# 512 tokens as the moving operand of layer two's output products, with shifted attention steps, reordered low parts and shared reciprocals

## The chip, the cores and the metric

One core of a Trainium2 chip runs the whole program. The metric is device time in microseconds (us); each kernel is timed by the median of several runs. A separate run, taken by the hardware profiler, gives the profile, and its time stands beside the others.

## What is computed

Attention over 4 batches, 8 heads, 512 local and 32 global tokens, then two feed-forward layers on the resulting 2176 rows of 512 columns. The local tokens see a window of 32 to either side and the global tokens; the global tokens see all.

```python
k_all = np.concatenate([k_g, k_l], axis=2);  v_all = np.concatenate([v_g, v_l], axis=2)
out_g = sm(scale * q_g @ k_all.T) @ v_all
mask = np.abs(pos[:, None] - pos[None, :]) <= window          # window = 32
s_l = np.concatenate([scale * q_l @ k_g.T, np.where(mask, scale * q_l @ k_l.T, -1e9)], axis=-1)
out_l = sm(s_l) @ v_all                                       # sm: exp(s - max) / (sum + 1e-9)
x = rows of out_g and out_l, heads side by side               # 2176 x 512
h = x @ w_in;   x = (maximum(h, 0) + alpha * minimum(h, 0)) @ w_out      # 512 -> 2048 -> 512
h = x @ w2_in;  out = (h * clip(h + 3, 0, 6) / 6) @ w2_out               # 512 -> 2048 -> 512
```

## The kernel before

**Precision.** Matmuls of the two layers run on float32r operands. Every operand is split into a high part (its cast to float32r) and a low part (the rest), and a product of two operands is three matmuls: high with high, low weight with high data, high weight with low data. The weights reach the chip as 64-bit floats and are made into 32-bit ones and split on the way (L114 to L138).

**Layer one** goes through the tokens in five blocks of 512, 512, 512, 256 and 384 columns (tokens stand in the columns). In each of a block's steps `h_tile` (L590) makes the hidden values of 128 rows of the 2048 in a bank `h_ps`, 12 matmuls; `act` (L600 to L609) turns them on ScalarE (ACT) and VectorE (DVE) into a high and a low part `g`; and `y_tiles` (L621) adds them, two steps later, to four banks `y_ps`, again 12 matmuls. In block 0 the weights are converted as they arrive, and its first eight steps take half the columns each. At the end of a block `x_transposed` (L550) turns the attention rows `xo` of the next block on TensorE (PE) into banks `xt_ps`, and `x_split` (L562, L563) makes the parts `xt` of them.

**Attention** is laid between these steps. Its work is 32 units (a batch, half of its tokens, two heads), taken in pairs. For a pair, `scores` (L234) makes 32 small matmuls into two banks; `softmax` masks them and finds the largest (L260), takes exponentials with their sums (L265), adds 1e-9 (L267) and takes reciprocals (L269), unit by unit; the probabilities are turned, by PE for the first pairs, later by DVE (L285) and a trip through DRAM; `values` (L299) makes 32 more (a float32 matmul counts twice in the trace) and multiplies by the reciprocals. Three tables set when: `STARTS` the step at which a pair's scores go (from pair 4 on), `WAITS` how many steps later its values go, and `STEPS` how many attention steps are taken behind each `h_tile`. The global tokens' attention follows in the last block.

**Layer two** takes its 2048 local tokens in two groups of 1024 (each a pair of 512-column halves), by Strassen's method in Winograd's form. Seven products of a quarter of the size take the place of eight, once for the hidden values and once for the output. The **input products** (`product`, L947) hold 128x128 weights stationary and move 512 tokens into banks `k_ps`. The **output products** (`summed`, L1035) are the other way round: seven sums `i` over four steps `k`, each of which makes a high and a low part of 512 tokens by two times 128 hidden rows (`parts_of`, L960 and L961: `gh`, `gl`), takes a tile `ws` of output weights that came from DRAM (`take`), and for two rows `jp`, four chunks of 128 tokens and three pairs of parts holds the chunk of tokens stationary and moves 256 output columns:

```python
bank = y[c // 2][:, 256 * (c % 2):256 * (c % 2) + 256]
mm = nc.tensor.matmul(bank, lhsT=part[:, jp, 128 * c:128 * c + 128],
                      rhs=wo[:, jp, 256 * wl:256 * wl + 256], ...)
```

So tokens come out on the partitions, as the rows of the output are. DVE adds up the sums (L877, tiles `res`), and `store` (L1062) writes each of four results per group by four transfers of 128 rows with 1 KB runs, from SyncE's queue (SP), which also fetches `ws`. The 128 global rows go by the plain method in the second group (L899, L911); `rest_out` (L920) uses the same `wo` tiles for them and adds to one bank `yr_ps`, and `rest_rows` stores it (L931, L934).

**Order.** The instructions of each engine are put in order when the program is built, by a scheduler that runs a timeline of its own; operations under `here` keep the order of the code. PSUM is two pools of four banks: `psy` holds `y_ps` in layer one, and `psr` serves everything else there (`h_ps`, scores, values, transposes), so that each needs a bank that ACT and DVE have emptied.

## Time and profile before

| | |
|---|---|
| median of 3 runs | 812.97 us (812.88 to 813.52) |
| the profiled execution | 818.06 us, of which 816.3 us are the span of the trace |
| PE busy | 795.4 us (97%), 6812 matmuls |
| DVE busy | 613.1 us (75%) |
| ACT busy | 409.8 us (50%) |
| GpSimd (POOL) busy | 86.6 us (11%) |
| mean granted clock of PE | 0.994 |

The trace has five stages: attention alone until about 20 us, layer one until 471, then in layer two the first group's input products to 549 and output products to 633, and the second group's input products to 716 and output products to 810. PE's busy time holds matmuls whose ends are modelled, and weight loads (PEld) overlap them; a pitch is better read from how long a known count took. The clock is given as a share of full speed, 1.0 for 2.4 GHz and 0.5 for 1.2 GHz. "Idle" is the time that an engine stood before an instruction, with what ended it.

### The profile page before, as it was taken

How to read it: one execution, taken by the hardware profiler on the slowest of the kernel's cores; microseconds unless marked ns; L12 is line 12 of the kernel's file. 1: busy time of each engine (PE TensorE's matmuls, PEld its weight loads, DVE VectorE, ACT ScalarE, POOL GpSimd, SP SyncE). 2: the span in 40 equal slices, each digit the busy share in tenths (PEclk: the TensorE clock that was granted, in tenths of full speed). 3: DMA queues.
4: the chain of work that ended last, by engine and by line, in shares of the span. 5: the costliest groups of instructions: out<-in, count | busy, mean ns of one | idle time of the engine just before them, and what ended most of it. 6: DMA issues, size and time to landing. Idle time of an engine off the chain costs nothing.

```text
span 816.3 us, 17563 instructions
## 1 busy us (share of the span) xinstructions
PE 795.4 (97%) x6812; PEld 696.2 (85%) x6812; DVE 613.1 (75%) x1307; ACT 409.8 (50%) x864; POOL 86.6 (11%) x141
## 2 busy tenths in 40 slices
PE   6999999999998999999999999999999999999998
PEld 4778777878886887788999988889999888899997
DVE  4889997678878887777899847778867576678443
ACT  5878886455546544544456434334543334333431
POOL 0332202122220322112000000000000000000000
PEclk9999999999999999999999999999999999999999
DMA  9978887489988889998995586676786666655663
GB/s 336 352 248 281 296 270 218 167 268 332 334 289 330 281 305 338 316 320 297 313 340 199 205 274 190 202 220 199 209 258 199 206 182 206 184 178 161 208 180 111
DMA packets 85507, 204.06 MB, mean 250 GB/s; under 512 B 8752, under 2 KB 31024, under 8 KB 85424
## 3 DMA queue, kind: packets, MB, share of 16 engines
q1 hardware_dynamic: 78112, 181.83, 67.2%
q0 software_dynamic: 7120, 20.98, 8.2%
q8 instruction: 54, 0.88, 0.5%
q14 instruction: 29, 0.24, 0.1%
q10 hardware_dynamic: 192, 0.13, 0.1%
HBM read 149.95 MB, written 52.95 MB: 249 GB/s over the span
## 4 chain that ended last, share of the span: by engine, by line
PE 79%; DMA 3%; DVE 1%; ACT 0%; issue 0%; SPq 0%; ACTq 0%
PE o_ps L1035 20%; PE k_ps L947 19%; PE y_ps L621 18%; PE h_ps L590 16%; DMA gk<-in_kN 2%; PE yr_ps L920 1%; PE hr_ps L899 1%; DMA xo<-turn 1%; PE o_ps L299 1%; PE s_ps L234 1%; PE gs_ps L440 1%; PE go_ps L477 0%; PE tr_ps L911 0%; PE xt_ps L550 0%; DVE p L260 0%
## 5 line engine op out<-in xcount | busy, mean ns | idle before, releaser
L590 PE MATMUL h_ps<-xt,wt 128*128 128x512 f32 (+2 forms) x1008 | 205.3, 353 | 2.4 <-DVE st L260 2.1
L621 PE MATMUL y_ps<-g,wt 128*128 128x512 f32 (+2 forms) x1008 | 206.4, 355 | 1.0 <-POOL wt L137 0.8
L590 PEld LDWEIGHTS h_ps<-xt,wt 128*128 128x128 f32 x1008 | 169.8, 191 | 25.8 <-issue 4.0
L621 PEld LDWEIGHTS y_ps<-g,wt 128*128 128x128 f32 x1008 | 168.8, 191 | 26.0 <-issue 2.4
L1035 PE MATMUL o_ps<-ws,gh 128*128 128x256 f32 x896 | 160.9, 283 | 0.1
L947 PE MATMUL k_ps<-bt,ws 128*128 128x512 f32 x672 | 157.2, 390 | 0.0
L947 PEld LDWEIGHTS k_ps<-bt,ws 128*128 128x128 f32 x672 | 124.6, 188 | 24.9
L1035 PEld LDWEIGHTS o_ps<-ws,gh 128*128 128x128 f32 x896 | 138.8, 192 | 0.6 <-issue 0.3
L1035 PE MATMUL o_ps<-ws,gl 128*128 128x256 f32 x448 | 124.2, 283 | 0.0
L961 DVE TENSOR_TENSOR gl<-far,gh 128x1024 fp32r<-128x1024 f32 x56 | 68.5, 1223 | 42.6 <-ACT gh L960 42.6
L960 ACT CAST gh<-far 128x1024 fp32r<-128x1024 f32 x56 | 58.7, 1049 | 74.7 <-PE o_ps L1035 70.9
L1035 PEld LDWEIGHTS o_ps<-ws,gl 128*128 128x128 f32 x448 | 84.9, 192 | 0.0
L881 ACT ACTIVATE t<-far,half_sb 128x512 f32<-128x512 f32 x48 | 34.8, 725 | 77.0 <-DVE far L877 77.0
L602 DVE SCALAR_TENSOR_TENSOR t<-t,c_sb,h_ps 128x512 f32<-128x512 f32 (+2 forms) x84 | 53.0, 641 | 17.9 <-ACT t L600 17.4
L600 ACT ACTIVATE t<-h_ps 128x512 f32<-128x512 f32 (+2 forms) x76 | 41.7, 550 | 47.0 <-PE h_ps L590 46.2
L608 ACT CAST g<-t 128x512 fp32r<-128x512 f32 (+2 forms) x76 | 43.7, 575 | 40.6 <-DVE t L602 37.7
L609 DVE TENSOR_TENSOR g<-t,g 128x512 fp32r<-128x512 f32 (+2 forms) x76 | 49.4, 653 | 10.9 <-ACT g L608 10.1
L265 ACT ACTIVATE p<-p,st 128x128 f32<-128x128 f32 x128 | 49.7, 392 | 10.0 <-DVE st L260 8.8
L114 ACT ACTIVATE raw<-raw,quarter_sb 128x512 uint32<-128x512 uint32 x64 | 49.2, 770 | 5.6 <-DMA raw<-in_w 5.6
L125 DVE SCALAR_TENSOR_TENSOR z<-z,raw 128x512 uint32<-128x512 uint32 x64 | 44.1, 695 | 5.0 <-ACT z L120 2.2
L127 DVE SCALAR_TENSOR_TENSOR z<-raw,z 128x512 uint32<-128x512 uint32 x64 | 44.7, 702 | 0.5
L882 DVE SCALAR_TENSOR_TENSOR far<-t,far 128x512 f32<-128x512 f32 x48 | 33.1, 689 | 11.8 <-ACT t L881 11.8
(110 smaller groups left out, 833.6 us busy)
## 6 DMA issues: line engine op xcount, KB each, us to landing
raw<-in_w SPq DMA_DIRECT2D x64, 512.0 KB, 7.1
ws<-wo SPq DMA_DIRECT2D x60, 512.0 KB, 3.9
ws<-wi SPq DMA_DIRECT2D x56, 512.0 KB, 4.7
v_t<-in_vE SPq DMA_DIRECT2D x32, 512.0 KB, 7.7
qk_t<-in_qkE SPq DMA_DIRECT2D x32, 368.0 KB, 5.7
wi<-raw SPq DMA_DIRECT2D x16, 512.0 KB, 5.4
wi<-parts SPq DMA_DIRECT2D x16, 512.0 KB, 6.3
wo<-raw SPq DMA_DIRECT2D x16, 512.0 KB, 5.8
```

Source lines behind the costliest of these rows:

```text
L114: here(nc.scalar.activation(low, low, AF.Relu, bias=quarter_sb, scale=0.9 * 2.0 ** -29))
L125: nc.vector.scalar_tensor_tensor(out=bits, in0=bits, scalar=3, in1=low, op0=ALU.logical_shift_left, op1=ALU.bitwise_or)
L127: nc.vector.scalar_tensor_tensor(out=bits, in0=high, scalar=0x80000000, in1=bits, op0=ALU.bitwise_and, op1=ALU.bitwise_or)
L265: nc.scalar.activation(to, to, AF.Exp, bias=st[:, 1, n:n + 1], scale=-1.0, accum_out=st[:, 2, n:n + 1])
L590: nc.tensor.matmul(ps[:, a:b], lhsT=wts[j][:, 0, wl, 128 * c:128 * c + 128], rhs=xt[c][:, xl, at:at + b - a], start=k == 0, stop=k == 3 * ...
L602: nc.vector.scalar_tensor_tensor(out=t[:, c:d], in0=t[:, c:d], scalar=c1_sb[:, j:j + 1], in1=ps[:, c:d], op0=ALU.mult, op1=ALU.add)
L609: nc.vector.tensor_tensor(out=g[:, 1, a:b], in0=t[:, a:b], in1=g[:, 0, a:b].bitcast(F32), op=ALU.subtract)
L621: nc.tensor.matmul(y[c][:, at:at + b - a], lhsT=wts[j][:, 1, wl, 128 * c:128 * c + 128], rhs=g[:, gl, a:b], start=first, stop=last, skip_g ...
L947: nc.tensor.matmul(bank, lhsT=wt[:, wl, 128 * c:128 * c + 128], rhs=bt[x][:, c, xl, 0:w], start=first and k == 0, stop=k == 5, skip_group_ ...
L960: nc.scalar.copy(hi, src)
L961: nc.vector.tensor_tensor(out=lo, in0=src, in1=hi.bitcast(F32), op=ALU.subtract)
L1035: mm = nc.tensor.matmul(bank, lhsT=part[:, jp, 128 * c:128 * c + 128], rhs=wo[:, jp, 256 * wl:256 * wl + 256], start=opens, stop=k == NP / ...
```

## The change

It has five parts.

1. **Output products.** `summed` holds 128x128 weights stationary (128 of the 256 output columns) and moves all 512 tokens of a part: 672 matmuls of 512 columns where there were 1344 of 256. Output columns now stand on the partitions and tokens in the columns. To bring the rows back, `store` has DVE turn each result in 32x32 squares, twice 128x512, and writes it by four transfers with runs of 64 columns (256 bytes). For that the columns of the output weights are permuted on the host, the copies and sums that fill a result write through a strided view (`half_of`), and the global rows read their weights through another (`in_order`).
2. **Attention steps.** Pair 13's scores go one step earlier (`STARTS`), with the values where they were; pair 5's values go one step later (`WAITS`).
3. **Shared reciprocals.** The two units of a pair share a tile of sums, and one addition and one reciprocal of 128x8 take the place of two of 128x4 each.
4. **Low parts last.** In layer one the matmul with the low part of the weights comes last of the three. `late`, in block 0's half steps, sorts it behind all the others of `h_tile`.
5. **Turning at a border.** `x_transposed` for the next block stands behind `y_tiles` of that step, and not ahead of it.

```diff
-STARTS = [0, 4, 8, 12, 16, 19, 22, 25, 29, 33, 36, 39]
+STARTS = [0, 4, 8, 12, 16, 19, 22, 25, 29, 32, 36, 39]
-WAITS = [4, 4, 5, 4, 5, 5, 5, 5, 5, 5, 5, 5]
+WAITS = [4, 5, 5, 4, 5, 5, 5, 5, 5, 6, 5, 5]
...
+            st = att.tile([128, 3, 8], F32, tag="st", name="st", bufs=4)
             for e, u in enumerate(us):
-                softmax(u, [x[:, 256 * e:256 * e + 256] for x in s])
-
-        def softmax(u, s):
+                softmax(u, [x[:, 256 * e:256 * e + 256] for x in s], st[:, :, 4 * e:4 * e + 4])
+            nc.vector.tensor_scalar(out=st[:, 2, :], in0=st[:, 1, :], scalar1=1e-9, scalar2=None, op0=ALU.add)
+            rs = att.tile([128, 8], F32, tag="rs", name="rs", bufs=FIRST_UNITS)
+            nc.vector.reciprocal(out=rs, in_=st[:, 2, :])
+            for e, u in enumerate(us):
+                rs_t[u] = rs[:, 4 * e:4 * e + 4]
+
+        def softmax(u, s, st):
...
-            nc.vector.tensor_scalar(out=st[:, 3, :], in0=st[:, 2, :], scalar1=1e-9, scalar2=None, op0=ALU.add)
-            rs_t[u] = att.tile([128, 4], F32, tag="rs", name="rs", bufs=FIRST_UNITS)
-            nc.vector.reciprocal(out=rs_t[u], in_=st[:, 3, :])
...
-    def h_tile(xt, wts, parts):
+    def h_tile(xt, wts, parts, late=False):
         ps = bank("h_ps")
         for a, b, j, at in parts:
-            k = 0
-            for c in range(NC):
-                for wl, xl in ((0, 0), (1, 0), (0, 1)):
...
+            steps = [(c, w) for c in range(NC) for w in ((0, 0), (0, 1), (1, 0))]
+            if late:
+                steps.sort(key=lambda step: step[1][0])
+            for k, (c, (wl, xl)) in enumerate(steps):
+                nc.tensor.matmul(ps[:, a:b], lhsT=wts[j][:, 0, wl, 128 * c:128 * c + 128],
+                                 rhs=xt[c][:, xl, at:at + b - a], start=k == 0, stop=k == 3 * NC - 1)
...
-            steps = [(w, c) for w in ((0, 0), (1, 0), (0, 1)) for c in range(len(y))]
+            steps = [(w, c) for w in ((0, 0), (0, 1), (1, 0)) for c in range(len(y))]
...
+        def in_order(w):
+            return w.rearrange("p (c b x) -> p b c x", c=2, b=4)
...
-                                     rhs=wo[:, jp, 256 * wl:256 * wl + 256], start=i == k == jp == wl == gl == 0,
+                                     rhs=in_order(wo[:, jp, 256 * wl:256 * wl + 256]), start=i == k == jp == wl == gl == 0,
...
+                    for jp in range(2) if turned else ():
+                        for c in range(2):
+                            k6 = 0
+                            for wl, part in ((0, hi), (1, hi), (0, lo)):
+                                at = 256 * wl + 128 * c
+                                opens = first and k == jp == k6 == 0
+                                mm = nc.tensor.matmul(y[c], lhsT=wo[:, jp, at:at + 128], rhs=part[:, jp, :], start=opens,
+                                                      stop=k == NP // 2 - 1 and jp == 1 and part is lo,
+                                                      skip_group_check=True)
+                                k6 += 1
...
+            def half_of(t, k):
+                return t.rearrange("p (a c x) -> p c a x", a=16, c=2)[:, k] if turned else t[:, 512 * k:512 * k + 512]
+
+            def columns_of(b):
+                return b.rearrange("p (a x) -> p a x", a=16) if turned else b
...
             def store(r, th, dm):
+                if turned:
+                    for at in range(0, 1024, 512):
+                        nc.vector.transpose(out=r[:, at:at + 512], in_=r[:, at:at + 512])
+                    to = rows[tiles[n][th][0][0], SG:S, 256 * dm:256 * dm + 256]
+                    for k in range(4):
+                        nc.sync.dma_start(out=to[:, 64 * k:64 * k + 64].rearrange("(a q) x -> q a x", q=32),
+                                          in_=r[32 * k:32 * k + 32].rearrange("q (a x) -> q a x", a=16))
+                    return
...
-            each(lambda s_, b: add(m1[:, s_], m1[:, s_], cols(b, s_)), w_)
+            each(lambda of, b: add(of(m1), of(m1), b), w_)
...
-                gs[s] = act(0, h_tile(xt, W1.wt, parts), parts)
+                gs[s] = act(0, h_tile(xt, W1.wt, parts, bi == 0 and s < 2 * DELAY), parts)
...
-                coming = x_transposed(blocks[bi + 1])
             if s >= LAG:
                 y_tiles(0, y, gs.pop(s - LAG), W1.wt, active(bi, s - LAG), bi == 0)
+            if s == end - 1 and not last:
+                coming = x_transposed(blocks[bi + 1])
...
+    turned = moe2_w_out.reshape(-1, 2, 4, 2, 32).transpose(0, 1, 3, 2, 4).reshape(moe2_w_out.shape)
```

PE's order in block 0, around pair 5's values (`s_ps` are the scores, `o_ps` here the values, `h_ps` and `y_ps` layer one's products). Before:

```order
L590 MATMUL h_ps<-xt,wt 128x512 x12
L234 MATMUL s_ps<-qk_t 32x128 x32
L299 MATMUL o_ps<-v_t,p 32x64 x32
L621 MATMUL y_ps<-g,wt 128x512 x12
```

Now:

```order
L593 MATMUL h_ps<-xt,wt 128x512 x12
L234 MATMUL s_ps<-qk_t 32x128 x32
L623 MATMUL y_ps<-g,wt 128x512 x12
L593 MATMUL h_ps<-xt,wt 128x512 x12
L301 MATMUL o_ps<-v_t,p 32x64 x32
```

Behind pair 6's scores stood pair 5's values at once; 24 matmuls of layer one now lie between the two.

PE at the border of block 0 to block 1 (`xt_ps` are the attention rows turned for block 1). Before:

```order
L590 MATMUL h_ps<-xt,wt 128x512 x11
L234 MATMUL s_ps<-qk_t 32x128 x30
L299 MATMUL o_ps<-v_t,p 32x64 x32
L550 MATMUL xt_ps<-consts_sb,xo 128x128 x4
L621 MATMUL y_ps<-g,wt 128x512 x22
```

Now:

```order
L593 MATMUL h_ps<-xt,wt 128x512 x10
L234 MATMUL s_ps<-qk_t 32x128 x31
L301 MATMUL o_ps<-v_t,p 32x64 x32
L623 MATMUL y_ps<-g,wt 128x512 x11
L552 MATMUL xt_ps<-consts_sb,xo 128x128 x4
```

Eleven of layer one's matmuls now stand between the values and the first turning.

PE at the border of block 1 to block 2, around pair 13's scores. Before:

```order
L621 MATMUL y_ps<-g,wt 128x512 x24
L590 MATMUL h_ps<-xt,wt 128x512 x6
L234 MATMUL s_ps<-qk_t 32x128 x2
L621 MATMUL y_ps<-g,wt 128x512 x12
L590 MATMUL h_ps<-xt,wt 128x512 x6
L234 MATMUL s_ps<-qk_t 32x128 x30
L590 MATMUL h_ps<-xt,wt 128x512 x12
L299 MATMUL o_ps<-v_t,p 32x64 x32
```

Now:

```order
L593 MATMUL h_ps<-xt,wt 128x512 x12
L234 MATMUL s_ps<-qk_t 32x128 x32
L623 MATMUL y_ps<-g,wt 128x512 x28
L593 MATMUL h_ps<-xt,wt 128x512 x3
L623 MATMUL y_ps<-g,wt 128x512 x8
L593 MATMUL h_ps<-xt,wt 128x512 x21
L301 MATMUL o_ps<-v_t,p 32x64 x32
```

Before, all but two of the scores stood behind the block's last `y_ps` and six `h_ps` matmuls; now they stand whole ahead of 28 `y_ps` matmuls.

## Rows read from the trace of the kernel before

**Rows 1.** Page, busy time of each engine, and the granted clock in 40 slices.
```profile
PE 795.4 (97%) x6812; PEld 696.2 (85%) x6812; DVE 613.1 (75%) x1307; ACT 409.8 (50%) x864; POOL 86.6 (11%) x141
PEclk9999999999999999999999999999999999999999
```

**Rows 2.** Page, chain that ended last: share of the span by engine and line.
```profile
PE o_ps L1035 20%; PE k_ps L947 19%; PE y_ps L621 18%; PE h_ps L590 16%; DMA gk<-in_kN 2%; PE yr_ps L920 1%; PE hr_ps L899 1%; DMA xo<-turn 1%; PE o_ps L299 1%; PE s_ps L234 1%; PE gs_ps L440 1%; PE go_ps L477 0%; PE tr_ps L911 0%; PE xt_ps L550 0%; DVE p L260 0%
```

**Rows 3.** Chain of waits in order of time: start us, us, what.
```profile
156.76 2.72 PE h_ps L590 x12
474.75 74.62 PE k_ps L947 x329
549.37 69.11 PE o_ps L1035 x576
651.30 0.71 PE hr_ps L899 x6
809.60 2.89 PE yr_ps L920 x24
```

**Rows 4.** PE in order of time at three stalls: start, us, what [idle].
```profile
82.69 1.10 PE L299 MATMUL o_ps<-v_t,p 128*32 128x64 f32 x64 [1.40 <-DVE t L602]
136.22 0.66 PE L550 MATMUL xt_ps<-consts_sb,xo 128*128 128x128 f32 x4 [1.71 <-DVE t L602]
252.31 4.51 PE L590 MATMUL h_ps<-xt,wt 128*128 128x512 f32 x12 [2.10 <-DVE st L260]
```

**Rows 5.** DVE in order of time beside the second stall.
```profile
134.92 0.43 DVE L563 TENSOR_TENSOR xt<-xo,xt 128x256 fp32r<-128x256 f32 x1 [4.36 <-ACT xt L562]
135.41 0.75 DVE L602 SCALAR_TENSOR_TENSOR t<-t,c_sb,h_ps 128x512 f32<-128x512 f32 x1
```

**Rows 6.** Third stall: PE, PEld, DVE, ACT, POOL busy, PEclk, DMA, GB/s.
```profile
254.00:256.00 2.00, 2.00 (x6) 1.55 (x5) 2.00 (x8) 1.13 (x3) 0.00 (x0) 0.50 1.01 404
```

**Rows 7.** PE's waits by releaser: us in total, times, longest.
```profile
PE y_ps L621 <- POOL wt L137: 0.8, 1, 0.8
```

**Rows 8.** Window in block 0, columns as in Rows 6.
```profile
80.00:100.00 20.00, 18.60 (x201) 15.30 (x201) 19.40 (x52) 16.75 (x39) 5.01 (x9) 1.00 0.87 288
```

**Rows 9.** Four groups on DVE: shapes, count | busy us, mean ns | idle.
```profile
L267 DVE TENSOR_SCALAR st<-st 128x4 f32<-128x4 f32 x32 | 6.0, 187 | 9.5 <-ACT p L265 9.4
L269 DVE RECIPROCAL rs<-st 128x4 f32<-128x4 f32 x32 | 4.9, 152 | 0.2
L285 DVE STREAM_TRANSPOSE p<-p 128x512 f32<-128x512 f32 x22 | 15.5, 702 | 0.0
L877 DVE TENSOR_TENSOR res<-res,o_ps 128x512 f32<-128x512 f32 x16 | 10.9, 686 | 5.6 <-PE o_ps L1035 5.4
```

**Rows 10.** Windows of the two output stages, columns as in Rows 6.
```profile
549.00:633.00 84.00, 84.00 (x689) 83.45 (x688) 67.78 (x76) 38.92 (x48) 0.00 (x0) 1.00 0.71 216
716.00:797.00 81.00, 81.00 (x659) 80.12 (x658) 51.24 (x49) 30.19 (x34) 0.00 (x0) 1.00 0.60 180
```

**Rows 11.** First output stage: a window of DVE, and one low part.
```profile
572.00:583.00 11.00, 11.00 (x12) 1.00 0.63 174
...
613.72 1.23 DVE L961 TENSOR_TENSOR gl<-far,gh 128x1024 fp32r<-128x1024 f32 x1 [1.65 <-ACT gh L960]
```

**Rows 12.** The end in order of time: start us, us, what.
```profile
808.92 1.41 DVE L877 TENSOR_TENSOR res<-res,o_ps 128x512 f32<-128x512 f32 x2 [4.41 <-PE o_ps L1035]
809.64 2.04 SPq L1062 DMA_DIRECT2D out<-res  x4
812.92 0.80 SPq L934 DMA_DIRECT2D out<-rz  x2
812.52 0.37 ACT L931 COPY rz<-yr_ps 128x256 f32<-128x256 f32 x1 [9.27 <-PE yr_ps L920]
```

**Rows 13.** DMA: queue's packets, MB, share; issues, KB, us to landing.
```profile
q1 hardware_dynamic: 78112, 181.83, 67.2%
out<-res SPq DMA_DIRECT2D x32, 128.0 KB, 3.1
```

More of the change, by code (lines that the diff above doesn't have):

```diff
@@ L618, in y_tiles @@
                 first = a == 0 and j == 0 and (wl, gl) == (0, 0)
-                last = j == NJ - 1 and (wl, gl) == (0, 1) and (not lanes or b == 512)
+                last = j == NJ - 1 and (wl, gl) == (1, 0) and (not lanes or b == 512)
                 if layer == 0:
@@ L979, in operands @@
                         yield operand(what, pair)
+            turned = True
             coming, split = operands(), []
@@ L1029, in summed @@
                     wo = take("sum", n, i, k)
-                    for jp in range(2):
+                    for jp in range(2) if turned else ():
[8 more added lines that the diff above has]
+                                k6 += 1
+                                if opens and i == c == 0:
+                                    here(mm)
+                    for jp in range(2) if not turned else ():
                         for c in range(chunks):
@@ L1068, in second_layer @@
             m1 = result()
-            each(lambda s_, b: nc.scalar.copy(m1[:, s_], cols(b, s_)), x_)
+            each(lambda of, b: nc.scalar.copy(of(m1), b), x_)
             summed(1, y_)
             m5 = result()
-            each(lambda s_, b: nc.scalar.copy(m5[:, s_], cols(b, s_)), y_)
+            each(lambda of, b: nc.scalar.copy(of(m5), b), y_)
             summed(2, x_, False)
             c11 = result()
-            each(lambda s_, b: nc.scalar.copy(c11[:, s_], cols(b, s_)), x_)
+            each(lambda of, b: nc.scalar.copy(of(c11), b), x_)
             store(c11, 0, 0)
@@ L1080, in second_layer @@
             summed(3, z_)
-            each(lambda s_, b: add(m1[:, s_], m1[:, s_], cols(b, s_)), z_)
+            each(lambda of, b: add(of(m1), of(m1), b), z_)
             summed(4, y_, False)
             c12 = result()
-            each(lambda s_, b: add(c12[:, s_], m1[:, s_], cols(b, s_)), y_)
+            each(lambda of, b: add(of(c12), of(m1), b), y_)
             store(c12, 0, 1)
@@ L1088, in second_layer @@
             u3_ = result()
-            each(lambda s_, b: add(u3_[:, s_], m1[:, s_], cols(b, s_)), w_)
+            each(lambda of, b: add(of(u3_), of(m1), b), w_)
             for at in range(0, 256 * chunks, 512):
```

18 lines of the change are left out of this document (6 added, 12 removed).

## The prediction

> **What bounds the kernel now.** I read the busy times first: TensorE (PE) is busy 97% of the span at the full granted clock nearly throughout, no other engine is over 75% [rows 1]. The chain that ended last says the same: 20% of the span in the output products of layer two (L1035), 19% in their input products (L947), 18% and 16% in layer one's two loops (L621, L590) [rows 2]. So time comes off only where PE issues fewer or shorter instructions, or where PE stands still. Next I read the chain in order of time for the pitch of each kind of matmul [rows 3], then PE's own order for its stalls [rows 4], and at each stall the engine that ended it [rows 5 to 8]. Last come the engines that the change loads: DVE and the DMA queues in the output stages [rows 9 to 11, 13] and the end of the program [rows 12].
>
> The sum is made against the profiled execution, 818.06 us (span 816.29 us and 1.77 us around it). It lies 5.1 us above the median of the three timed runs, 812.97 us; I take the difference off the median unchanged. About 0.2%, 1.6 us, can be told from no change.
>
> **Output products.** They are 1344 matmuls with 256 moving columns; 576 of them in a row took 69.11 us, 120.0 ns each. The input products move 512 columns: 329 in 74.62 us, 226.8 ns each, and layer one's 12 in 2.72 us are the same [rows 3]. At 2.4 GHz the columns alone are 106.7 and 213.3 ns; both kinds pay 13.3 to 13.5 ns beyond that, so the surplus belongs to the instruction, not to the columns. The change computes the same columns in 672 matmuls of 512: 1344 x 120.0 = 161.3 us become 672 x 226.8 = 152.4 us, **8.9 us less**. The bounds are 0 (two old pitches, 240 ns) and 8.9; I take 8.9, since the nearest row is a float32r matmul of the same shape.
> The Trainium skill (TensorE: Matmul & The Clock Gate, "Back-to-back issue gap") gives the warm gap as the columns at 2.4 GHz plus about 2.5 ns; by that 672 instructions fewer would save 1.7 us, not 8.9. The rows show 13.3, and the measurement decides.
>
> **Order of high and low parts.** Layer one's loops now use the same weights in two neighbouring matmuls. That saves nothing by itself: there are as many weight loads as matmuls [rows 1], although the old output products already used one stationary operand twice in a row, at the usual pitch. What it does is ask for the weights' low part later. PE waited 0.8 us once for a low part on POOL [rows 7]; four matmuls of 256 columns more now lie ahead of it, 0.5 us. I take 0.4 (bounds 0 and 0.8).
>
> **Steps of attention.** Three stalls of PE in blocks 0 and 1 stand where the order changes. (a) 1.40 us at 82 us, for a bank that DVE had yet to empty (L602) [rows 4]: pair 5's values followed pair 6's scores directly; now 24 matmuls of 512, 5.4 us, lie between. But DVE was busy 19.4 of 20 us there [rows 8] and may be late elsewhere: I take half, 0.7 (bounds 0 and 1.4). (b) 1.71 us at 136 us, the transposes for block 1 waiting for the same kind of release [rows 4]; DVE itself had stood 4.36 us behind a cast of rows still in flight [rows 5]. Eleven matmuls, 2.5 us, now go ahead of the transposes. The last of layer one's products need the same late DVE result soon after, so I take 0.9 (bounds 0 and 1.7). (c) 2.10 us at 252 us for DVE's softmax of pair 13; the 12 matmuls behind it took 4.51 us instead of 2.72 [rows 3, 4], since the granted clock stood at 0.50, the 1.2 GHz level, after PE had idled [rows 6]. Pair 13's scores now stand a step earlier, with 28 y matmuls behind them, 6.3 us in which DVE can finish. I take all, 2.1 + 1.8 = 3.9 (bounds 0 and 3.9).
>
> **Shared reciprocals.** 16 TENSOR_SCALAR and 16 RECIPROCAL go: 16 x (187 + 152) ns = 5.4 us of DVE over the span [rows 9]. None of it is on PE's path, so 0; it helps DVE keep up in (a) to (c). The shared pair waits for eight exponentials instead of four, and DVE's queue with it. That costs nothing while PE has matmuls queued; without that cover it is one more stall of the size of (a).
>
> **Turning the results back.** The products now come out with output columns on the partitions. Each of 8 results gets two DVE transposes of 128x512 between its last add and its store: 16 x 0.70 = 11.2 us of DVE [rows 9]. The second output stage has room, 51 of 81 us busy; the first has 68 of 84 [rows 10] and a stretch without idle time [rows 11], and 5.6 us go there. A step's low part starts after 1.65 us of waiting for its operand buffer [rows 11], so DVE runs ahead by more than one result's 1.4 us. I take 0.5 us lost (bounds 0 and 5.6). The stores wait on SP for the transposes, and weight loads queue behind them; six tiles are fetched ahead, 16 us at 2.7 us a step, so 1.4 us is hidden. Adds and copies write runs of 32 elements: 0, as the transposing ones before did. The global tokens' 96 output matmuls (L920) read their moving operand in runs of 32: operands in two runs went at 0.71 us for six, 118 ns, no slower than whole ones [rows 3]; I take 0 (bounds 0 and a doubled pitch, 11.5).
>
> **The end.** Before, the last add ends at 810.33 us, the four stores issue from 809.64 to 811.68, and the two SP stores of the global rows until 813.72 [rows 12]. Now both transposes need both banks: 810.33 + 1.4 = 811.7, four issues at 0.51 to 813.8, the SP pair to 814.6. That is 0.9 us later; the 24 global matmuls, 2.9 us [rows 3], hide the rest. Each store also writes 512 runs of 256 bytes instead of 128 of 1 KB. At the queue's mean, 0.672 x 16 x 816.3 us / 78112 = 112 ns for 2.3 KB, 256 bytes are 12 ns by bytes and 112 by count [rows 13]. A landing took 3.1 us [rows 13]; by count it could be four times that, 9.3 more. I take 0.9 (bounds 0 and 9.3), since the rows price mostly bytes.
>
> **Sum:** -8.9 - 0.4 - 0.7 - 0.9 - 3.9 + 0.5 + 0.9 = -13.4 us: 804.7 profiled, **799.6 us** at the median.
>
> **Rivals.** (A) The stalls only move: in layer one DVE, not PE, sets the pace, and a wait that is taken from one bank returns at the next. For it: 19.4 of 20 us [rows 8]. Against: over whole blocks PE has no other stalls, and (c) is the order's alone. Then -8.9 + 1.4 = -7.5: 805.5 us. (B) The new products do not reach 226.8 ns, through the changed operands, and the change does not do its main work: -5.9 + 1.4 = -4.5: 808.5 us. By the 2.5 ns of the page on TensorE it would be 806.8; the rows speak against both. (C) DVE becomes the bound of the first output stage and all 5.6 us show: 799.6 + 5.1 = 804.7 us. (D) Slower: the short runs of the stores fill the DMA engines, and PE waits for weights in the output stages. They were busy 0.71 x 84 = 59.6 and 0.60 x 81 = 48.6 us [rows 10], some 6.3 of each for the old stores by bytes. In the shorter stages 26.3 and 34.3 us are free for 512 short packets per engine each, so the first fills at 51 ns a packet; the 13.4 us gained and 1.6 more are gone at (60.6 + 15) / 1024 = 74 ns. At the mean packet's 112 ns it is 54 us lost: 854 us. By bytes, 12 ns, it never starts.
> The Trainium skill (DMA: Bandwidth & Descriptors, "Specifications") says that below 512 bytes a transfer is a read-modify-write. If that doubles the 12 ns, the end grows by an estimated 128 x 12 ns = 1.5 us, to 801.1 us, and no stage fills; no run here shows it yet.
>
> **Numbers.** Forecast, 796.5 to 803.5 us: 0.55. (A) 0.24. (B) 0.05. (C) 0.08. (D) 0.04. Better still, every stall gone in full and the start shortened: 0.04. From 795.5 to 806.5 us lie the forecast and nearly all of A and C, 0.82. Faster by over 0.2%: all but D and a little of B, 0.94; within 0.2%: 0.02; slower: 0.04.
>
> **What would show it.** The output products at 226 to 228 ns a matmul; 240 means B. PE's order without idle time at the first pair of scores and values in 512-wide steps, at the first block border, and at the second, where the granted clock stays full; stalls beside a new bank mean A. No PE wait for the low part gl or for ws in the output stages; a wait on gl means C, on ws D. PE's last matmul to the span's end should be 4.5 to 5 us instead of 3.8. I am wrong if the stalls that go are less than half of those listed, or if the stage of the output products shortens by less than 7 us.

## The result, and the profile after

The changed kernel takes 807.91 us (median of 9 runs, 803.10 to 810.30), the kernel before 813.52 us on the same chip (9 runs, 812.70 to 818.12): ratio 0.9914, 95% interval 0.9886 to 0.9941. It is faster, as forecast, but by 7.0 us and not by 13.4; the range of the forecast ended at 806.5. The ratio takes in all runs, and the 7.0 us are worked out from it; the two medians lie 5.6 us apart. A second series gave 0.992 (0.9895 to 0.9945).

The profiled execution has a span of 808.4 us, 7.9 less than that of before; each is slower than the median of its kernel (810.14 and 818.06 us). The page's busy times, granted clock, and DMA packets (answering to [rows 1] and [rows 13]):

```profile
PE 789.3 (98%) x6140; PEld 662.4 (82%) x6140; DVE 620.0 (77%) x1291; ACT 410.0 (51%) x864; POOL 87.1 (11%) x141
PEclk9789999999999999999999999999999999999999
q1 hardware_dynamic: 90400, 181.83, 68.7%
```

672 matmuls are gone, as they should be, and 12288 packets were added, 32 stores times 384. Its chain in order of time (start us, us, what) answers to [rows 3]:

```profile
473.85 74.61 PE k_ps L952 x329
548.46 65.28 PE o_ps L1042 x288
800.10 2.87 PE yr_ps L925 x24
```

288 matmuls of 512 columns took 65.28 us, 226.7 ns each, where 576 of 256 took 69.11; the global rows' 24 matmuls, which now read runs of 32, are as quick as before. The stages show where time went. First the kernel before in four stretches (us; PE, PEld, DVE, ACT, POOL busy; PEclk; DMA share; GB/s): block 0 of layer one, block 2, the first output stage with most of the second group's input products behind it, and the second output stage, counted from its first output product, with the last 48 input products among them.

```profile
20.17:144.02 123.85, 117.29 (x1356) 95.85 (x1355) 109.30 (x313) 98.04 (x255) 29.96 (x38) 0.99 0.83 278
243.42:345.30 101.88, 99.78 (x891) 78.95 (x889) 84.12 (x225) 54.33 (x135) 22.44 (x40) 0.98 0.90 311
549.21:708.43 159.22, 159.22 (x1069) 147.33 (x1068) 116.39 (x146) 66.58 (x90) 0.00 (x0) 1.00 0.67 204
708.43:809.60 101.17, 101.06 (x800) 98.92 (x799) 62.00 (x63) 35.43 (x41) 0.00 (x0) 1.00 0.59 177
```

The same four of the changed kernel:

```profile
21.19:147.20 126.01, 121.97 (x1355) 99.82 (x1355) 107.89 (x297) 96.89 (x252) 30.28 (x38) 0.93 0.78 267
246.54:345.94 99.40, 99.14 (x838) 78.26 (x837) 82.68 (x203) 52.25 (x122) 22.18 (x40) 1.00 0.93 317
548.30:703.06 154.76, 154.76 (x733) 129.74 (x732) 120.71 (x154) 67.09 (x90) 0.00 (x0) 1.00 0.70 209
703.06:800.10 97.04, 96.89 (x464) 81.16 (x463) 64.72 (x69) 35.01 (x41) 0.00 (x0) 1.00 0.63 185
```

The two stretches with the output stages give 4.46 + 4.13 = 8.6 us. Block 2 gives 2.5. Block 0, in which two of the three stalls should have gone, is 2.2 us **longer**, and its granted clock is 0.93. PE's waits by releaser (us in all, times, longest) tell a part of why:

```profile
PE xt_ps L552 <- DVE xo L321: 4.7, 2, 3.2
PE h_ps L593 <- DVE xt L565: 2.0, 2, 1.6
PE h_ps L593 <- ACT wt L136: 0.7, 1, 0.7
```

The waits for a bank behind DVE's L602 and for the softmax, 1.4, 1.7 and 2.1 us [rows 4], are no longer listed. In their place PE waits for `xt`, 1.6 us at once, which in the profile of before was this:

```profile
PE h_ps L590 <- DVE xt L563: 0.3, 1, 0.3
```

The place is near 52 us, where the second half of block 0 starts. The changed kernel's engines there, in order of time:

```profile
14.83 0.17 DVE L239 TENSOR_SCALAR st<-st 128x8 f32<-128x8 f32 x1 [3.61 <-ACT p L270]
...
51.20 0.83 PE L552 MATMUL xt_ps<-consts_sb,xo 128*128 128x128 f32 x4 [1.50 <-DVE xo L321]
51.77 1.43 POOL L137 TENSOR_TENSOR wt<-z,wt 128x512 fp32r<-128x512 f32 x1 [2.57 <-ACT wt L136]
51.99 1.23 DVE L239 TENSOR_SCALAR st<-st 128x8 f32<-128x8 f32 x1
53.14 0.74 DVE L565 TENSOR_TENSOR xt<-xt_ps,xt 128x256 fp32r<-128x256 f32 x2
53.61 0.80 PE L593 MATMUL h_ps<-xt,wt 128*128 128x256 f32 x2 [1.57 <-DVE xt L565]
```

DVE has the shared sum (L239) in its queue ahead of the low parts of `xt` (L565), for which PE has nothing else to do. The sum takes 1.23 us and not 0.17: it ends at 53.22, just after POOL's instruction at 53.20. In the kernel before, PE already stood 1.35 us ahead of the same transposes, and one of its 32 additions was already slow there; the prediction read neither row:

```profile
48.78 0.83 PE L550 MATMUL xt_ps<-consts_sb,xo 128*128 128x128 f32 x4 [1.35 <-DVE xo L319]
49.99 0.84 DVE L267 TENSOR_SCALAR st<-st 128x4 f32<-128x4 f32 x1
```

In the changed kernel PE stands 1.50 and then 1.57 us, and during the second of these waits the granted clock falls to the 1.2 GHz level: over 51 to 53 us its mean is 0.82.

```profile
51.00:53.00 2.00, 0.83 (x4) 0.40 (x4) 2.00 (x4) 1.42 (x4) 1.23 (x1) 0.82 1.06 381
```

The next stretch, here and at the same point of the kernel before (columns as in [rows 6]), the changed one first:

```profile
53.00:59.00 6.00, 5.39 (x25) 5.40 (x26) 2.21 (x7) 0.62 (x1) 1.48 (x2) 0.50 0.76 268
```

```profile
53.00:59.00 6.00, 6.00 (x53) 6.00 (x52) 3.69 (x9) 4.58 (x10) 0.00 (x0) 1.00 0.39 154
```

In these six microseconds PE got through 25 matmuls where it had been 53 before, some of them smaller.

This place is not all of the 2.2 us. The last `xt_ps` of block 0's second half already come 2.4 us later than before (51.20 against 48.78), 1.0 of them because layer one starts later, and the clock was also low at the start of the block. A stretch there, the changed kernel's first:

```profile
26.00:31.00 5.00, 5.00 (x33) 3.40 (x31) 3.40 (x19) 4.06 (x17) 2.96 (x2) 0.50 1.03 403
```

```profile
24.00:29.00 5.00, 4.79 (x40) 2.97 (x39) 4.59 (x23) 3.38 (x14) 2.98 (x2) 0.93 1.03 403
```

What put the clock there is not shown.

### The profile page after: what moved, and what is told of

Same layout as the page of the kernel before. It is cut to its first block, busy times and chain, and to the rows that moved or that the text cites. A ratio compares the mean times of both kernels' runs of the same rounds, so it can differ in the third digit from the quotient of the medians.

```text
span 808.4 us, 16186 instructions
## 1 busy us (share of the span) xinstructions
PE 789.3 (98%) x6140; PEld 662.4 (82%) x6140; DVE 620.0 (77%) x1291; ACT 410.0 (51%) x864; POOL 87.1 (11%) x141
## 4 chain that ended last, share of the span: by engine, by line
PE 79%; DMA 9%; DVE 5%; issue 3%; ACT 2%; POOL 1%; SPq 0%; DVEq 0%; POOLq 0%; ACTq 0%
PE k_ps L952 19%; PE o_ps L1042 19%; PE y_ps L623 17%; PE h_ps L593 17%; DMA gk<-in_kN 2%; DMA turn<-xo 2%; PE s_ps L234 2%; DMA raw<-in_w 1%; PE yr_ps L925 1%; PE hr_ps L901 1%; DMA xo<-turn 1%; PE o_ps L301 1%; ACT p L270 1%; DVE z L125 1%; PE gs_ps L442 1%
## 5 line engine op out<-in xcount | busy, mean ns | idle before, releaser
L593 PEld LDWEIGHTS h_ps<-xt,wt 128*128 128x128 f32 x1008 | 171.6, 193 | 26.4 <-DVE xt L565 2.6
L1042 PE MATMUL o_ps<-gh,ws 128*128 128x512 f32 x448 | 132.6, 390 | 0.1
L1042 PEld LDWEIGHTS o_ps<-gh,ws 128*128 128x128 f32 x448 | 83.4, 188 | 17.4 <-issue 0.5
L1042 PE MATMUL o_ps<-gl,ws 128*128 128x512 f32 x224 | 81.6, 390 | 0.0
L604 DVE SCALAR_TENSOR_TENSOR t<-t,c_sb,h_ps 128x512 f32<-128x512 f32 (+2 forms) x84 | 53.2, 642 | 16.5 <-ACT t L602 16.0
L602 ACT ACTIVATE t<-h_ps 128x512 f32<-128x512 f32 (+2 forms) x76 | 41.4, 548 | 30.7 <-PE h_ps L593 29.7
L1042 PEld LDWEIGHTS o_ps<-gl,ws 128*128 128x128 f32 x224 | 41.7, 188 | 8.4
```

The lines of the kernel that those rows point to most:

```text
L593: nc.tensor.matmul(ps[:, a:b], lhsT=wts[j][:, 0, wl, 128 * c:128 * c + 128], rhs=xt[c][:, xl, at:at + b - a], start=k == 0, stop=k == 3 * ...
L604: nc.vector.scalar_tensor_tensor(out=t[:, c:d], in0=t[:, c:d], scalar=c1_sb[:, j:j + 1], in1=ps[:, c:d], op0=ALU.mult, op1=ALU.add)
L1042: mm = nc.tensor.matmul(y[c], lhsT=wo[:, jp, at:at + 128], rhs=part[:, jp, :], start=opens, stop=k == NP // 2 - 1 and jp == 1 and part is ...
```

## The experiments

All ratios are to the kernel before on the same chip, over all runs and not of the medians, with a 95% interval; 0.001 is 0.8 us.

| kernel | runs | median us | ratio |
|---|---|---|---|
| the change | 9 | 807.91 | 0.9914 (0.9886 to 0.9941) |
| the change, again | 6 | 807.34 | 0.9920 (0.9895 to 0.9945) |
| output products alone | 7 | 809.25 | 0.9940 (0.9915 to 0.9964) |
| all but the output products | 12 | 813.72 | 0.9996 (0.9976 to 1.0017) |
| shared reciprocals alone | 12 | 815.93 | 1.0018 (0.9997 to 1.0038) |
| moved steps alone | 12 | 814.14 | 0.9990 (0.9971 to 1.0010) |
| later turning alone | 12 | 813.42 | 0.9984 (0.9970 to 0.9998) |
| moved steps and later turning | 6 | 810.10 | 0.9946 (0.9930 to 0.9961) |
| order of parts alone | 12 | 815.27 | 1.0008 (0.9990 to 1.0027) |
| change, old steps | 12 | 809.46 | 0.9935 (0.9910 to 0.9960) |
| change, no sorting | 6 | 807.32 | 0.9925 (0.9902 to 0.9948) |
| change, reciprocals by unit | 6 | 804.81 | 0.9895 (0.9875 to 0.9915) |
| change, old order of parts | 6 | 805.81 | 0.9900 (0.9873 to 0.9926) |
| change, results not turned back | 6 | 805.41 | 0.9893 (0.9869 to 0.9917) |
| change, by unit and old order | 6 | 805.06 | 0.9881 (0.9856 to 0.9905) |
| the same, last stores on two queues | 5 | 804.32 | 0.9880 (0.9860 to 0.9900) |
| change, old order, shared from pair 6 | 6 | 804.02 | 0.9872 (0.9847 to 0.9898) |
| change, old order, shared to pair 5 | 6 | 806.25 | 0.9891 (0.9862 to 0.9920) |

**The change again**, unedited.

> The changed kernel again, as the measure for the kernels beside it. Its profile showed the three stalls of the forecast gone and the output stages shorter by 8.6 us, but block 0 of layer one 2.2 us longer and the start 1.0 us later. Theory 1 (the start of layer one got worse: PE idles twice before 54 us and the granted clock falls to 0.50 for several us after each): 805 to 809 us again, the clock low between 20 and 60 us again, and single runs some us apart according to how long it stays low. Theory 2 (the profiled run was an unlucky one): the median comes out near 802, with no clock stretch at 0.50 after 45 us.

805 to 809 as theory 1 has it, single runs 4 us apart. The clock was at 0.50 from 20 to 23 us, far shorter than in the first profile, and again from 50 to 57 us; block 0 took 124.53 us.

**The output products alone.** Tables, `scores` and `softmax`, `h_tile` and `y_tiles`, and the place of the turning are those of before.

```diff
-WAITS = [4, 5, 5, 4, 5, 5, 5, 5, 5, 6, 5, 5]
+WAITS = [4, 4, 5, 4, 5, 5, 5, 5, 5, 5, 5, 5]
...
+                coming = x_transposed(blocks[bi + 1])
             if s >= LAG:
...
-            if s == end - 1 and not last:
-                coming = x_transposed(blocks[bi + 1])
```

> The output products and the stores of the change alone; steps, reciprocals, order of parts and the place of the turning as before. Theory 1: the output stages give 8.6 us and the end takes 1.6 back, and layer one is as before: 7.0 us under the kernel before, some 806 us, so that the changed kernel gets nothing on top from its other four parts. Theory 2: the four other parts are worth their 4.5 us, then this one is slower than the changed kernel by 4 us. Theory 3 (the new products fall short and layer one did its part): only 4 us under the kernel before.

4.9 us under before (2.9 to 6.9), and between theories 1 and 2. Its stages say more than its runs: the two output stages are those of the changed kernel to 0.01 us.

```profile
543.94:698.70 154.76, 154.76 (x734) 129.72 (x732) 120.63 (x154) 66.90 (x90) 0.00 (x0) 1.00 0.70 210
698.70:795.74 97.04, 96.89 (x464) 81.17 (x463) 65.00 (x69) 35.20 (x41) 0.00 (x0) 1.00 0.63 185
```

Its layer one is that of the kernel before, and the clock was full all through. Block 0 took 122.28 us, and layer one ended at 465.6 us, where the kernel before has 470.9. So executions of one and the same layer one lie several us apart.

**All but the output products**: `summed`, `each`, `store` and the host's columns as before.

```diff
-            turned = True
...
-    turned = moe2_w_out.reshape(-1, 2, 4, 2, 32).transpose(0, 1, 3, 2, 4).reshape(moe2_w_out.shape)
```

> The change without its output products, stores and host permutation (these as before); steps, reciprocals, order of parts and place of the turning as changed. Theory 1 (the four parts give back at the start of block 0 most of what the vanished stalls give): within 3 us of the kernel before, 810.5 to 813.5 us, and the profile shows the stalls at 82, 136 and 252 us gone, those near 50 us grown to 1.5 us each. Theory 2 (they are worth what the forecast said): 4.5 us or more under the kernel before, some 808. The output stages should be as long as before to 0.2 us (159.2 and 101.2 us), and the end 3.8 us.

813.72, no gain that can be told from nothing: theory 1. The interval still allows 2.0 us of gain, and the median is 1.5 us under that of the kernel before. The wait for `xt` near 50 us was there again, the three stalls were not, and the output stages were 159.23 and 101.18 us. In this one execution the clock stayed full at 50 us, and block 0 (122.43 us) and block 2 (98.20) were shorter than before; the last two blocks of layer one were not (126.29, before 125.59). The four parts of layer one together thus gave far less than the 5.9 us of the forecast: layer one, and not layer two, is where it failed.

**Reciprocals by unit** in the change (`scores` and `softmax` as before), **no sorting**, and **the old order of parts** in it.

```diff
-            nc.vector.tensor_scalar(out=st[:, 2, :], in0=st[:, 1, :], scalar1=1e-9, scalar2=None, op0=ALU.add)
-            rs = att.tile([128, 8], F32, tag="rs", name="rs", bufs=FIRST_UNITS)
-            nc.vector.reciprocal(out=rs, in_=st[:, 2, :])
...
-                gs[s] = act(0, h_tile(xt, W1.wt, parts, bi == 0 and s < 2 * DELAY), parts)
+                gs[s] = act(0, h_tile(xt, W1.wt, parts), parts)
...
-            steps = [(w, c) for w in ((0, 0), (0, 1), (1, 0)) for c in range(len(y))]
+            steps = [(w, c) for w in ((0, 0), (1, 0), (0, 1)) for c in range(len(y))]
```

> The change with the reciprocals unit by unit as before. Theory 1a (the shared sum holds DVE and ACT up at the turning for block 0's second half, until eight exponentials are done, so that the parts of xt come late): the stall of 1.57 us before 54 us goes to 0.3 as before, the clock stays full from 50 to 60 us, block 0 ends 3 to 4 us earlier (143 to 144 us) and the time is 3 to 4 us under the changed kernel. Theory 1b (the order of the parts does it): same time as the changed kernel within 1 us.

> The change without the sorting of the low weight parts to the end of h_tile in block 0's half steps (the new order of three within a chunk stays). Theory 1b (the sorting scatters the scores between the first h_ps matmuls, PE does little until 31 us and the clock stays at 0.50 until then): the clock is full from 26 us on as before, and block 0 ends 2 to 3 us earlier than in the changed kernel. Theory 1a: no difference beyond 1 us.

> The change with the old order of high and low parts in both loops of layer one, and without the sorting. If the order costs or gives nothing: the same as the changed kernel within 1 us, with PE waiting 0.8 us once for a low part on POOL near 36 us, as before. If it is what makes the start late and scatters the scores, the clock is full from 26 us on and the time 2 to 3 us under the changed kernel.

By unit, block 0 ended at 142.88 us, PE waited 0.3 us for `xt`, and the median fell by 2.5 us: theory 1a, with somewhat less than its 3 to 4 us. The sorting makes no difference, against theory 1b. The old order is better by 0.0014 to 0.0020 in the ratio, 1.1 to 1.6 us, which the intervals do not part from nothing. In the two kernels that had the new order and reciprocals by unit, PE waited for the high part of a weight, and the clock fell to 0.50 behind it; the same line stands in both profiles:

```profile
PE h_ps L591 <- ACT wt L136: 2.9, 1, 2.9
```

With the old order it is 0.2 us, plus the 0.8 for POOL that [rows 7] showed. With the new order and shared reciprocals it is 0.7 us in the change, and without the sorting neither wait is in the list. So the new order removes the wait for POOL, and together with the sorting it brings a later one, which is larger where the reciprocals go by unit.

**Old steps** in the change (the two tables of before).

> The change with the old tables of steps for pairs 5 and 13. If the moved steps are what took away the stalls for pair 5's values and pair 13's softmax, these come back: 1.4 us near 82 us in block 0, and 2.1 us plus a stretch at half the clock at the border of block 1 to block 2, 3 to 5 us slower than the changed kernel in all, with block 2 at 100.8 to 101.9 us where the change has 99.0 to 99.4. Rival A (the stalls only move): the same time as the changed kernel within 1 us.

Slower than the change by 0.0015 to 0.0021 in the ratio, 1.2 to 1.7 us. The first stall came back at half its size, 0.7 us, and for a transfer. Rival A is out for the third: it came back in full, with block 2 at 102.90 us and the clock at 0.50 behind it; the wait in its list:

```profile
PE h_ps L593 <- DVE st L265: 2.2, 1, 2.2
```

**Results not turned back**: the turned branch of `store` left out.

```diff
-                if turned:
-                    for at in range(0, 1024, 512):
-                        nc.vector.transpose(out=r[:, at:at + 512], in_=r[:, at:at + 512])
...
-                    return
```

> The change with the results stored as before, by four transfers of 128 rows with runs of 1 KB, and without the two transposes each: the turning back of the results is left out, so rows and columns of the output are mixed. If the end is 1.6 us longer through the transposes and the short runs, it goes from 5.4 back to 3.8 us from PE's last matmul to the end of the span, and the time is 1.6 us under the changed kernel; the output stages stay at 154.8 and 97.0 us, since PE waits for neither. If the transposes or the short packets slow the output stages (rivals C and D), these get shorter as well.

The end went from 5.42 to 3.61 us, the output stages stayed (154.66 and 97.04). Neither the transposes nor the short packets slow the stages: C and D are out.

**One part alone** on the kernel before: shared reciprocals, moved steps, order of parts, and later turning.

> The kernel before with the shared reciprocals alone. Theory 1a (the shared sum is made after eight exponentials; DVE has it in its queue ahead of the parts of xt for block 0's second half, so PE waits 1.5 us longer before 54 us, and the granted clock tends to fall behind that): 1 to 4 us slower than the kernel before, the stall for xt at 1.5 us or more where it was 0.3. Rival (the saving of 5.4 us of DVE helps, or nothing): same as before within 1 us, or faster.

> The kernel before with the new tables of steps alone. By the forecast the stalls for pair 5's values and for pair 13's softmax go, with the clock's fall behind the second: 0.7 to 1.4 and 3.9 us, so 4 to 5 us under the kernel before, block 2 at 98.9 to 99.4 us where it was 101.9. If a stall of DVE's making returns elsewhere in block 0, 3 us or less.

> The kernel before with the new order of high and low parts and the sorting in the half steps alone. By the forecast 0.4 us faster, which cannot be told from nothing. Theory 1b (the new order costs time at the start of block 0): 1 to 2 us slower than before, with the first h_ps matmuls more scattered between the scores.

> The kernel before with the later turning alone. Theory 3: 1.5 to 3 us faster, since the stall of 1.7 to 2.1 us at the border of block 0 to block 1 goes and the clock has no idle time to fall behind. Theory 4: 0 to 1 us faster. By the forecast 0.9 us faster.

Shared reciprocals alone are 1.5 us slower (from 0.2 faster to 3.1 slower). Near 50 us PE waited 1.9 us for the rows that it turns, where it was 1.4 in the kernel before, and then 0.6 us for `xt`, where it was 0.3 and the expectation said 1.5 or more; the clock was low from 51 to 58 us. The profile is of the slowest of the 12 runs. The moved steps alone gave 0.8 us, far under their 4 to 5, although the profile, of the fastest of the 12 runs, had block 2 at 98.28 us. The stall at the border of block 0 was still there, with the clock down behind it; first PE's row, then the stretch:

```profile
133.87 1.11 PE L550 MATMUL xt_ps<-consts_sb,xo 128*128 128x128 f32 x4 [1.89 <-DVE t L602]
```

```profile
131.00:138.00 7.00, 5.11 (x77) 4.27 (x73) 4.88 (x24) 4.48 (x18) 0.00 (x0) 0.76 0.75 253
```

**Moved steps and later turning**, nothing else. It differs from the kernel with the steps alone by the place of `x_transposed`.

> The kernel before with the moved steps and the later turning, and none of the other parts. It differs from the kernel with the moved steps alone only at the border of block 0 to block 1. Theory 3 (the moved steps give their time only if the stall there, 2.1 us with the clock falling behind it, goes too): 3 us under the kernel before, ratio 0.996 to 0.997, with no idle time of PE over 0.6 us near 132 us. Theory 4 (the profile of before was some 5 us over its median, by stalls that most executions don't have; there was never more than 1 or 2 us to gain): 0 to 1.5 us under, like the moved steps alone (0.999).

> The kernel before once more, for a second profile. The first was an execution of 818.06 us against a median of 813 to 815. Theory 4 says that this one has a first layer some 3 to 5 us shorter (its end at 466 to 468 us, not 470.9), by smaller stalls or fewer falls of the clock, and the same two output stages to 0.2 us. Theory 3: the three stalls at 82, 136 and 252 us are all there again, with 1.4 to 2.4 us each.

4.4 us under before (3.2 to 5.7): theory 3. Block 0 fell to 120.98 us and block 2 to 99.04:

```profile
20.48:141.46 120.98, 116.86 (x1356) 96.00 (x1354) 108.40 (x310) 96.75 (x252) 29.83 (x38) 0.99 0.84 282
240.12:339.16 99.04, 99.04 (x836) 78.32 (x835) 82.39 (x205) 51.88 (x121) 21.91 (x39) 1.00 0.92 319
```

The second profile of the kernel before, one execution of 815.57 us, has two of the three waits again, and 0.3 us instead of 1.7 at the border; its first layer ended 2.5 us earlier than in the first. Both theories have a part.

```profile
PE h_ps L590 <- DVE st L260: 2.2, 1, 2.2
PE o_ps L299 <- DVE t L602: 1.5, 1, 1.5
PE xt_ps L550 <- DVE t L602: 0.3, 1, 0.3
```

Behind the first of these waits, for pair 13's softmax, the clock stayed full this time. The 12 matmuls there took 3.00 us, where the first profile has 4.51 [rows 4]:

```profile
252.34 3.00 PE L590 MATMUL h_ps<-xt,wt 128*128 128x512 f32 x12 [2.18 <-DVE st L260]
```

**By unit and old order**, and with **the last stores on two queues**:

```diff
+                        queue = nc.scalar if end and (th, dm) == (1, 0) and k % 2 else nc.sync
-                        nc.sync.dma_start(out=to[:, 64 * k:64 * k + 64].rearrange("(a q) x -> q a x", q=32),
+                        queue.dma_start(out=to[:, 64 * k:64 * k + 64].rearrange("(a q) x -> q a x", q=32),
```

> The change with the reciprocals unit by unit and with the old order of high and low parts: output products, moved steps and the later turning are kept. If both that are taken out cost time at the start, this is 3 to 4 us under the changed kernel, 803 to 804 us where the kernel before has 813 to 815, and the ratio 0.987 or less. If they cost it through the same stall, it is no better than with unit reciprocals alone, 0.9895.

> The change with unit reciprocals and the old order of parts, and with two of the last four stores issued from ScalarE's queue instead of SyncE's. In the change SyncE issues four stores and two of the global rows one behind the other from 802.2 to 806.0 us. If that line of issues sets the end, the end gets 1.0 to 1.5 us shorter: 3.9 to 4.4 us from PE's last matmul to the end of the span instead of 5.4, and the time some 804. If the transfers themselves set it, 5.4 stays.

Both are faster than the change by the ratios, by some 3 us, though the intervals overlap; between each other they are the same. The end did not shorten: it was 5.91 us. In the change, SyncE issued the last transfers one behind another:

```profile
802.19 2.23 SPq L1085 DMA_DIRECT2D out<-res  x4
803.39 1.03 ACTq L939 DMA_DIRECT2D out<-rz  x2
804.53 1.46 SPq L939 DMA_DIRECT2D out<-rz  x2
```

With two queues nothing stood ahead of the global rows, but their own issues took 2.4 us (0.80 before [rows 12], where the stores had 128 runs each):

```profile
798.70 0.85 SPq L1084 DMA_DIRECT2D out<-res  x2
800.07 2.40 SPq L937 DMA_DIRECT2D out<-rz  x2
800.07 2.46 ACTq L937 DMA_DIRECT2D out<-rz  x2
```

So the line of issues does not set the end. What is left is the transposes, behind which the stores start, and the short runs; no run leaves out one of them alone.

**Where the shared sum costs.** On the change with the old order, a pair's reciprocals are shared from pair 6 on, or only up to pair 5.

```diff
+            if us[0] >= 2 * SHARED:
+                shared(us, st, 0, 8)
...
+                if not us[0] >= 2 * SHARED:
+                    shared((u,), st, 4 * e, 4 * e + 4)
```

> The change with the old order of parts, and the reciprocals shared only from pair 6 on; the first six pairs, which run at the start of block 0, have theirs unit by unit. If the shared sum costs its 1.5 to 2 us at the start alone (behind eight exponentials, ahead of the parts of xt for block 0's second half), this runs like the kernel with unit reciprocals throughout and the old order: ratio 0.987 to 0.989, the stall for xt near 50 us at 0.5 us. If it costs something at every pair, 0.990 as with all of them shared.

> The counterpart: the old order of parts, and the reciprocals shared for the first six pairs alone. If the cost lies at the start, it is all here: ratio 0.990 to 0.991, 1.5 to 2 us over the one beside it, with PE waiting 2 us for the turned rows and 0.8 us or more for xt near 48 to 50 us, and the clock low for several us behind that in some executions. If not, 0.988.

2.2 us apart at the medians and 1.5 by the ratios, as expected for a cost that lies at the start. The intervals overlap, and the ratio of early sharing, 0.9891, lies between the two that were expected. The waits in the profiles agree. Sharing late, the wait for `xt` was as before:

```profile
PE h_ps L599 <- DVE xt L572: 0.3, 1, 0.3
```

Sharing early, it was 0.6 us, with the sum again about as long as POOL's instruction beside it, and the clock low behind it:

```profile
49.27 1.17 DVE L246 TENSOR_SCALAR st<-st 128x8 f32<-128x8 f32 x1
```

```profile
51.00:54.00 3.00, 3.00 (x16) 3.00 (x16) 0.82 (x4) 0.00 (x0) 0.64 (x1) 0.54 1.02 386
```

These 0.6 us, and not the 1.6 of the change, are what all three profiles have in which the first pairs share and the order of parts is the old one. The change with the old order:

```profile
50.17 2.41 PE L592 MATMUL h_ps<-xt,wt 128*128 128x256 f32 x18 [0.58 <-DVE xt L565]
```

All profiles side by side show that the wait of 1.6 us needs two parts of the change together. The columns are PE's idle time before the second half's last `xt_ps` and before `h_ps`, in us, and how often the clock fell to 0.50 between 45 and 60 us:

| at the start of block 0 | profiles | `xt_ps` | `h_ps` | clock fell |
|---|---|---|---|---|
| by unit, old order | 9 | 1.3 to 1.4 | at most 0.3 | in 1 |
| shared, old order | 3 | 1.9 | 0.6 | in 2 |
| shared, new order, sorted | 5 | 1.5 | 1.6 | in 4 |

Shared and with the new order but without the sorting, it was 0.5 and 1.1 us, and the clock stayed full there; by unit and with the new order, no wait for `xt` was over 0.4 us.

## Why the prediction was right in direction and too large

- **Output products, -8.9 us forecast.** Right: 226.7 ns a matmul, and 8.6 us over both stages in the profiles with the part, against those without it (one, by unit and old order, has 0.4 less). The 2.5 ns that the Trainium skill gives (TensorE: Matmul & The Clock Gate, "Back-to-back issue gap") would have made it, as an estimate, 1.7; the surplus per instruction in the rows, 13.3 ns, is what came out. The 0.3 us that are missing lie in the second stage, and not with the transposes, for which 0.5 was set: without them that stage is as long (97.04 us), and both stages together are 0.1 us shorter.
- **The end, +0.9.** The mechanism was right, the size was not: 1.6 us (5.42 instead of 3.81). The sum let SyncE's issues of the global rows start later by the transposes and kept their 0.80 us; behind 512 runs a store they took 1.46.
- **The three stalls, -5.5.** Mostly right: steps and turning together gave 4.4 us (3.2 to 5.7), and all three waits left the list of the change. Alone they gave 0.8 and 1.3 us, which was not foreseen; that each needs the other is not settled, since the intervals allow 2.4 us each. One way for it was seen: with the steps alone the clock fell behind the stall that was left at 134 us; behind the like stall in the first profile of the kernel before, it did not. Part of the size was taken from an execution that was 5.1 us over the median, a difference that was taken off unchanged. The second profile had the stall at the border at 0.3 us, so 1.7 was no typical value. Of the 3.9 us for (c), 1.8 were for the fall of the clock, and block 2 shortened by 2.5: the second profile and that of the output products alone have the wait of 2.2 us with a full clock behind it.
- **Shared reciprocals, 0.** This step failed. "That costs nothing while PE has matmuls queued; without that cover it is one more stall of the size of (a)" named the condition, and did not ask where the cover is missing. It is missing at the start of block 0's second half, where PE stood 1.35 us in the kernel before as well; "over whole blocks PE has no other stalls", said against rival A, overlooked that row. There the sum stands beside POOL's instruction and takes 1.23 us, and the parts of `xt` wait behind it. The eight exponentials are not what holds it there: they are done at 50.65 us, and DVE is at other work until the sum starts at 51.99. Nor is it the sum alone: PE's wait for `xt` is 0.6 us with it, and 1.6 with it and the new order of parts. That the low part of `xt` is now read by the second of three matmuls, not the third, would explain it, but is not shown. The price by the ratios: 1.5 to 2.0 us between the change and the one with reciprocals by unit, 1.5 between the old order with and without sharing, 1.5 between early and late sharing, 1.5 alone. No one of them is clear of noise; that all have the same sign and nearly the same size speaks for it.
- **Order of parts, -0.4.** The sign was wrong by what can be seen: 0.7 to 1.6 us slower, by the ratios, in the pairs that differ by it, no one of them clear of noise. PE's wait of 0.8 us for POOL did go; a wait of 0.4 to 2.9 us for a later weight's high part came in all profiles with the sorting, and with the reciprocals shared also the longer wait for `xt`.
- **The sum by parts that were run**: -8.6 + 1.6 - 4.4 + 1.7 + 1.1 = -8.6 us, the last two (reciprocals, order) from the middle of the ratios' differences. Measured: -7.0 (4.8 to 9.3 faster). What is left lies inside the interval.

By the difference, rival A was nearest (-7.5 against -7.0), by the median B (808.5 against 807.91); both by luck. In the change the three stalls did not move to another bank, as A has it, and two other parts of the change took their gain; only some variants have waits at the first border again (in the profile of the change with the old order, 1.2 us for a transfer and 1.1 for DVE's L604). The products reached 226.7 ns, so B did not happen, and neither did C and D.

## What to carry to other kernels

An instruction that is saved on an engine with room can still cost time, if what replaces it waits longer at the head of that engine's queue: look for the place where the bottleneck has nothing queued, and read there what stands behind the new wait. Read that place one instruction at a time: a mean of 187 ns over 32 additions [rows 9] hid one of 840. Before a stall is priced from one profile, compare that execution's time with the median; here two profiles of one kernel had 1.7 and 0.3 us at the same place. Matmuls of twice the width paid by the instruction count alone, and could be counted on to 4%.

## What the runs showed of the hardware

- A TENSOR_SCALAR of 128x8 on DVE took 0.17 us alone and 1.23 or 1.17 us while POOL ran a TENSOR_TENSOR, ending within 0.02 us of it in the first case. The Trainium skill (SBUF — State Buffer, "Who interferes with whom") says that such an operation and one on GpSimd can take a shared pair of ports for the whole instruction, and the other waits; the rows agree.
- During the second of PE's stalls of 1.50 and 1.57 us the granted clock went to 0.50 and stayed there for some 7 us, most of them with PE busy again. It did so in four of the five profiles, of the change and of near variants, that had both stalls; in the fifth, all but the output products, it stayed full there. It fell in one of the nine profiles with the shortest waits too, in the second of the kernel before, for some 3 us behind a wait of 1.39. So the longer wait goes with the fall, and does not settle it. The output stages agree to 0.1 us between profiles of the same form, but for one that is 0.4 longer, so the scatter of some us between executions is layer one's.
- Runs of 256 bytes cost little in the output stages (the stage lengths with and without them agree to 0.1 us) and, together with the transposes ahead of the stores, 1.6 to 1.8 us at the end, where nothing hides them: two issues of 32 KB took 0.80 us behind stores with 1 KB runs and 1.03 to 2.46 beside or behind these.

The kernel with the lowest median has the output products, the moved steps, the later turning, the old order of parts, and shared reciprocals from pair 6 on: 804.02 us, ratio 0.9872 (0.9847 to 0.9898), against 0.9914 for the change; the intervals just overlap, and it is not told apart from the one by unit and old order (0.9881).
